# Moving the mix for the gate into the attention part, and splitting the gate's last steps over slots

## The chip, the cores and the metric

The kernel runs on one core of one Trainium2 chip. The metric is the time of one execution on the device, in microseconds, as the median of several runs. The engines are named as the profile names them: PE (TensorE), DVE (VectorE), ACT (ScalarE), POOL (GpSimd) and SP (SyncE, which issues most DMAs here).

## The reference

```python
# attention: batch 8, 12 heads, 448 positions, head size 64
scores = cap * np.tanh(scale * np.matmul(q, k.transpose(0, 1, 3, 2)) / cap)
attn = np.exp(scores - np.max(scores, axis=-1, keepdims=True))
attn = attn / (np.sum(attn, axis=-1, keepdims=True) + 1e-09)
x = np.matmul(attn, v)           # then heads joined: x is (8, 448, 768)
# channel mix
x_prev = np.concatenate([np.zeros((B, 1, D)), x[:, :-1, :]], axis=1)
xk = mu_k * x + (1.0 - mu_k) * x_prev
xr = mu_r * x + (1.0 - mu_r) * x_prev
k = np.maximum(xk @ w_k, 0.0)    # w_k is 768 x 1024
v = k * k @ w_v                  # w_v is 1024 x 768
r = 1.0 / (1.0 + np.exp(-(xr @ w_r)))   # w_r is 768 x 768
return r * v
```

The result of the attention is the x of the second part. Each position is mixed with the position before it, once with mu_k for the keys and once with mu_r for the gate r.

## The kernel before

The kernel works in three stages, one after the other on PE, each engine executing its instructions in the order in which the program was written.

**Attention and keys** (about the first 575 us). There are 48 pairs of heads. Iteration i of the loop calls the steps named in the string STEP one by one, for pair i or a pair one or two behind it. For a pair, PE makes the scores (scores, the tiles s), ACT takes tanh and exp of them (the tiles p), DVE sums them per 32 rows (red, L238), and PE multiplies them with the values (values, the tile pv). The partial sums are gathered by four small DMAs (gather, L243), added and inverted on DVE (recip, L247 to L251), stored and loaded again as a row for all partitions (rec_store, rec_load), and norm (L263) multiplies pv by it: this gives x, 128 features by 448 positions, in one of two tiles. mix_old (ACT, L273) and mix_new (DVE, L278) make xk from x; x_high and x_low (POOL, L74 and L84) split xk into two parts xkh and xkl, from which PE makes the key products seven iterations later (kpart, L313; K in STEP). relu and k_store write them to DRAM as k_d. x_store writes x to DRAM as x_d. Also in this loop, the 44 pieces of the weights are converted: five DVE operations a piece (f in STEP, L372 to L380), one on POOL (L387), and DMAs (weight_load, weight_store to w_d). Iterations 6 to 10 take two pieces, others one, up to about iteration 39.

**Value units** (to about 795 us). v = (k * k) @ w_v is made in 14 units of 256 positions. A unit is a product of 2 x 2 blocks made with seven block products instead of eight (P1 to P7); each of them is a slot. The left operand of a product is a block of the source tile src or a sum or difference of blocks (sums2, on POOL, the tiles s). operand, two slots ahead, splits it into hi (ACT, L553) and lo (DVE, L554), in a ring of three buffers. PE multiplies hi by the high and the low part of the weights and lo by the high part. evacuate then adds the products up from PSUM: p1 (ACT), u2 and u3 (DVE, L588), and four results per unit (DVE, L592, or ACT, for the one that is complete in PSUM), which go to DRAM as v_d. The weights' own blocks and sums are made by w2_prep: those for w_v in the last six iterations of the first loop, those for w_r during the value units.

**Gate units** (to the end). r = sigmoid(xr @ w_r) is made in the same way, in 14 units of seven slots with nine matmuls each. The source is made on the way: src_r_load reads x with the position ahead of it (the tile xc), and src_r, ten slots ahead, multiplies the earlier position by 1 - mu_r (on POOL or ACT in turns, L514 and L516) and adds mu_r times the later one (DVE, L517). In evacuate, ACT applies the sigmoid to each result (L599), POOL multiplies by the value (L600, in the last unit DVE), and SP stores to the output.

A slot wrote its instructions in the order evacuation of the slot before, matmuls, work ahead:

```python
        if g:
            v, r = divmod(g - 1, SLOTS)
            self.evacuate(v, self.products(v)[r])
        if u < 2 * NU:
            self.multiply(u, s)
            self.ahead(g)
```

Of the kernel before, what the change touches and what calls it, by code (L numbers as in the profile page):

```python
# [17 lines left out]
NP = H // 2  # L18
# [33 lines left out]
weight_sum tanh1 exp1 red1 norm recip rec_store K qk_high qk_low tanh2 mix_old mix_new x_high x_low relu k_store  # L52
K exp2 red2 weight_rest weight_sum relu k_store S3 K K tanh3 exp3 red3 relu k_store weight_abs load_qk rec_load x_store weight_store"""
# [6 lines left out]
class Body:  # L60
# [227 lines left out]

    def x_store(self, i):
        self.nc.sync.dma_start(self.x_d[i % NP, :, i // NP, :], self.X[i % 2])  # L290
# [148 lines left out]
    def w2_prep(self, kind):  # L439

        lo = self.W2[kind][1]
        sub = self.nc.gpsimd.tensor_sub
# [24 lines left out]
    def src_v_load(self, u, q):  # L467
        if q == 0:
            self.src[u] = self.srcp.tile([P, NF, 2 * P], F32, name="src")
        self.nc.sync.dma_start(self.src[u][:, 2 * q:2 * q + 2, :],  # L470
                               self.k_d[2 * q:2 * q + 2, :, u * 2 * P:(u + 1) * 2 * P].rearrange("f p t -> p f t"))

    def src_v(self, u, q):
        x = self.src[u][:, 2 * q:2 * q + 2, :]
        self.nc.vector.tensor_mul(x, x, x)  # L475

    def pieces(self, u):

        b, s0 = divmod((u - NU) * 2 * P, S)
        cut = S - s0  # L480
        out = []
        for c in range(2):
            k = cut - c * P
            if k <= 0 or k >= P:
                out.append((c * P, c * P + (k <= 0), P, 1))
            else:
                assert 2 * k == P
                out.append((c * P, c * P, k, 2))
        if out[0][3] == out[1][3] == 1:
            gap = out[1][1] - P  # L490
            return [(0, 0, 2 * P, 1, 0)] if not gap else [(0, 0, P, 2, P + 1)]
        return [(o, i, k, a, k + 1) for o, i, k, a in out]

    def src_r_load(self, u, q):
        b, s0 = divmod((u - NU) * 2 * P, S)
        w = 2 * P + 1 + (s0 + 2 * P > S)
        o = b * (S + 1) + s0
        t = self.xc[u, q] = self.ldp.tile([P, 2 * P + 2], F32, name="xc", bufs=4)
        self.nc.sync.dma_start(t[:, 0:w], self.x_d.rearrange("c p b s -> c p (b s)")[q, :, o:o + w])

    def src_r(self, u, d):
        nc = self.nc
        if d == 0:
# [319 lines left out]
```

## Time and profile before

| | |
|---|---|
| median of 3 runs | 1057.7 us (1057.36 to 1057.74) |
| profiled execution | 1057.44 us |
| its span, first to last instruction | 1055.3 us |
| granted PE clock over the span | 0.955 |
| busy: PE, DVE, ACT, POOL | 930.4, 804.4, 614.2, 576.3 us |

A row of the timeline reads: start in the span, duration, engine, line of the kernel, operation, output and input by the program's names, shapes, count, and in brackets how long the engine sat idle before it and for whom. A row of the groups has the count, then busy us and mean ns of one, then idle time before and its releasers. The chain is the work that ended last, followed back from the end. PEld is PE's loading of weights, SPq and ACTq are the queues on which those engines issue DMAs.

### The profile page before, as it was taken

What the parts mean: (1) busy time and instruction counts of PE and PEld (TensorE: products, weight loads), DVE (VectorE), ACT (ScalarE), POOL (GpSimd) and SP (SyncE); (2) the same over time, 40 slices, a digit from 0 to 9 for tenths busy, and PEclk for the clock granted to TensorE, in tenths of its full rate; (3) what the DMA queues carried; (4) which work ended last, traced back from release to release, by engine and by line L of the source; (5) the groups of instructions that cost most, each with busy time, mean ns of one, the idle gap of its engine ahead of it and who ended that gap; (6) DMA issues with size and microseconds to landing.
All of it is one profiled execution on the core that took longest, in us unless ns stands there. A gap on an engine that the chain in (4) does not pass through costs nothing.

```text
span 1055.3 us, 15510 instructions
## 1 busy us (share of the span) xinstructions
PE 930.4 (88%) x4986; PEld 738.6 (70%) x4986; DVE 804.4 (76%) x1285; ACT 614.2 (58%) x941; POOL 576.3 (55%) x504
## 2 busy tenths in 40 slices
PE   7788989999999999999987999999997667667667
PEld 3345756676767676676666999999997656657556
DVE  7999988878878888766645889999686576575664
ACT  7886768878888888877734343443344333333332
POOL 4756565655556465544145456454466565665662
PEclk9888999999999999999988899999998988998988
DMA  5565556565666656554253544344434344343342
GB/s 155 168 186 186 170 169 214 194 200 192 211 208 204 201 193 211 175 166 129 99 190 130 162 147 123 107 131 131 150 114 145 103 129 128 104 141 116 115 130 92
DMA packets 119546, 164.06 MB, mean 155 GB/s; under 512 B 23072, under 2 KB 103584, under 8 KB 119456
## 3 DMA queue, kind: packets, MB, share of 16 engines
q1 hardware_dynamic: 110240, 148.30, 45.2%
q10 hardware_dynamic: 9216, 14.68, 3.8%
q8 instruction: 41, 0.67, 0.3%
q14 instruction: 49, 0.40, 0.1%
HBM read 106.76 MB, written 53.41 MB: 152 GB/s over the span
## 4 chain that ended last, share of the span: by engine, by line
PE 55%; DVE 14%; issue 11%; POOL 10%; ACT 6%; DMA 2%; SPq 1%; DVEq 0%; ACTq 0%; POOLq 0%
PE ps L569 20%; PE kps L313 16%; PE s L194 9%; PE pv L221 8%; DVE src L517 3%; DVE r L238 3%; POOL src L514 3%; ACT p L212 2%; POOL s L537 2%; PE pv L229 2%; POOL s L533 2%; DVE o L592 1%; ACT p L202 1%; DVE lo L554 1%; POOL o L600 1%
## 5 line engine op out<-in xcount | busy, mean ns | idle before, releaser
L238 DVE TRANSPOSE_TENSOR_REDUCE r<-p 128x28 f32<-128x896 f32 (+1 forms) x240 | 220.1, 922 | 76.2 <-ACT p L212 71.9
L202 ACT ACTIVATE p<-s,scl_t 128x896 f32<-128x896 f32 x192 | 173.4, 903 | 44.6 <-PE s L194 37.0
L212 ACT ACTIVATE p<-p,cap_t 128x896 f32<-128x896 f32 x192 | 182.0, 948 | 10.2 <-ACT ko L320 5.5
L569 PE MATMUL ps<-wrh,hi 128*128 128x384 f32 x294 | 110.4, 375 | 75.9 <-DVE u L588 25.6
L313 PE MATMUL kps<-xkh,wkh 128*128 128x448 f32 x384 | 147.7, 385 | 12.4 <-ACT ko L320 12.4
L313 PE MATMUL kps<-xkl,wkh 128*128 128x448 f32 x384 | 141.9, 370 | 0.5 <-POOL xkl L84 0.5
L313 PE MATMUL kps<-xkh,wkl 128*128 128x448 f32 x384 | 142.0, 370 | 0.0
L569 PE MATMUL ps<-wvh,hi 128*128 128x384 f32 x392 | 132.9, 339 | 4.5 <-ACT hi L553 4.5
L569 PE MATMUL ps<-wvl,hi 128*128 128x384 f32 x392 | 132.4, 338 | 0.0
L387 POOL TENSOR_TENSOR wsq<-wa,wsq 128x384 f32<-128x384 f32 x44 | 44.3, 1007 | 155.9 <-DVE wsq L380 128.1
L221 PE MATMUL pv<-p,rv 128*64 128x448 f32 x576 | 126.6, 577 | 0.0
L569 PEld LDWEIGHTS ps<-wrh,hi 128*128 128x128 f32 x294 | 61.0, 208 | 89.2 <-ACT hi L553 32.5
L84 POOL TENSOR_TENSOR qkl<-rqk,qkh 128x960 fp32r<-128x960 f32 x47 | 106.0, 2256 | 3.9
L554 DVE TENSOR_TENSOR lo<-src,hi 128x512 fp32r<-128x512 f32 (+1 forms) x84 | 79.9, 951 | 36.9 <-ACT hi L553 36.2
L554 DVE TENSOR_TENSOR lo<-s,hi 128x512 fp32r<-128x512 f32 (+1 forms) x112 | 91.0, 813 | 20.3 <-ACT hi L553 20.3
L569 PE MATMUL ps<-wrl,hi 128*128 128x384 f32 x294 | 106.4, 362 | 0.0
L194 PE MATMUL s<-qkh 64*128 64x448 f32 (+1 forms) x336 | 84.6, 444 | 22.6 <-ACT p L202 17.9
L553 ACT CAST hi<-s 128x512 fp32r<-128x512 f32 (+1 forms) x112 | 63.2, 564 | 66.1 <-PE ps L569 47.8
L313 PEld LDWEIGHTS kps<-xkh,wkh 128*128 128x128 f32 x384 | 73.6, 192 | 33.5 <-ACT ko L320 15.3
L600 POOL TENSOR_TENSOR o<-o,vl 128x384 f32<-128x384 f32 x52 | 53.1, 1020 | 74.2 <-ACT o L599 73.5
L194 PEld LDWEIGHTS s<-qkh 64*128 64x128 f32 (+1 forms) x336 | 37.2, 190 | 78.9 <-ACT p L202 28.5
L533 POOL TENSOR_TENSOR s<-src 128x512 f32<-128x512 f32 (+1 forms) x28 | 36.0, 1287 | 103.2 <-DVE src L475 83.8
(95 smaller groups left out, 1968.7 us busy)
## 6 DMA issues: line engine op xcount, KB each, us to landing
rqk<-qk SPq DMA_DIRECT2D x47, 480.0 KB
k_d<-ko ACTq DMA_DIRECT2D x64, 224.0 KB
src<-k_d SPq DMA_DIRECT2D x56, 256.0 KB
rv<-v SPq DMA_DIRECT2D x48, 256.0 KB
x_d<-x SPq DMA_DIRECT2D x48, 224.5 KB
r<-rec_d SPq DMA_DIRECT2D x96, 112.0 KB
v_d<-o SPq DMA_DIRECT2D x56, 192.0 KB
vl<-v_d SPq DMA_DIRECT2D x56, 192.0 KB
```

Source lines behind the costliest of these rows:

```text
L84: {"p": self.nc.gpsimd, "v": self.nc.vector}[e].tensor_sub(*a)
L194: nc.tensor.matmul(s[:, h, 0:S], qk[a][p, k], qk[b][p, 0:S], start=(n == 0), stop=(n == 2))
L202: self.nc.scalar.activation(p32, self.S.pop((i, g))[:, :n, 0:S], AF.Tanh, scale=self.scl_t)
L212: self.nc.scalar.activation(p32, p32, AF.Exp, scale=1.0 if self.maxima else self.cap_t)
L221: nc.tensor.matmul(pv[p, 0:S], v[:, g, h, :], ph[:, h, :], start=(g == 0), stop=False)
L238: self.nc.vector.tensor_reduce(out=out, in_=p32[p, h].rearrange("p h (b k) -> p (h b) k", k=32), axis=mybir.AxisListType.X, op=ALU.add, ap ...
L313: nc.tensor.matmul(self.kps[fc][:, 0:S], w, m[:, dc, :], start=first, stop=last)
L533: pool.tensor_add(s, a(1, 0), a(1, 1))
L553: self.nc.scalar.copy(hi, x)
L554: self.nc.vector.tensor_sub(lo, x, f(hi))
L569: self.nc.tensor.matmul(o, a[:, c, :], w[:, c, :], start=first and k == 0, stop=last and k == len(todo) - 1, skip_group_check=True)
L600: (nc.vector if u == 2 * NU - 1 else nc.gpsimd).tensor_mul(o, o, self.vl.pop((u, key)))
```

## The change

- gate_old (POOL) and gate_new (DVE) make xr, mixed, in the attention loop, in one tile xg, for the pair two behind. They stand after x_low and after red3 in STEP. x_store writes xg instead of x; x_d loses the column for the position ahead of the first.
- The gate units load their source like the value units, three loads of 256 KB a unit; src_r_load, src_r and pieces go.
- A slot writes the matmuls and the work ahead first, then the evacuation of the slot before. The last steps go to a list that is carried out one slot later: the copy and store of a value, and for the gate the sigmoid, into PSUM (tile psg, two buffers), and another slot later the multiplication, now on DVE, with the store.
- The value is loaded two slots ahead of the unit's slot instead of one, into six buffers instead of three.
- The subtractions of w2_prep go from POOL to DVE, for both kinds.

```diff
-weight_sum tanh1 exp1 red1 norm recip rec_store K qk_high qk_low tanh2 mix_old mix_new x_high x_low relu k_store
-K exp2 red2 weight_rest weight_sum relu k_store S3 K K tanh3 exp3 red3 relu k_store weight_abs load_qk rec_load x_store weight_store"""
+weight_sum tanh1 exp1 red1 norm recip rec_store K qk_high qk_low tanh2 mix_old mix_new x_high x_low gate_old relu k_store
+K exp2 red2 weight_rest weight_sum relu k_store S3 K K tanh3 exp3 red3 gate_new relu k_store weight_abs load_qk rec_load x_store weight_store"""
+    def gate_old(self, i):
+        hp = i % NP
+        self.xg = self.up.tile([P, S], F32, name="xg", bufs=1)
+        self.nc.gpsimd.tensor_scalar(self.xg, self.X[i % 2][:, 0:S], self.om["r"][:, hp:hp + 1], None, op0=ALU.mult)
+    def gate_new(self, i):
+        self.nc.vector.scalar_tensor_tensor(out=self.xg, in0=self.X[i % 2][:, 1:], scalar=self.mu["r"][:, i % NP:i % NP + 1],
+                                            in1=self.xg, op0=ALU.mult, op1=ALU.add)
     def x_store(self, i):
-        self.nc.sync.dma_start(self.x_d[i % NP, :, i // NP, :], self.X[i % 2])
+        self.nc.sync.dma_start(self.x_d[i % NP, :, i // NP * S:(i // NP + 1) * S], self.xg)
...
-        sub = self.nc.gpsimd.tensor_sub
+        sub = self.nc.vector.tensor_sub
...
+    def src_load(self, u, q):
...
+        if 2 * q < 2 * self.half(u):
+            x, t = (self.k_d, u) if u < NU else (self.x_d, u - NU)
+            self.nc.sync.dma_start(self.src[u][:, 2 * q:2 * q + 2, :],
+                                   x[2 * q:2 * q + 2, :, t * 2 * P:(t + 1) * 2 * P].rearrange("f p t -> p f t"))
...
-            nc.scalar.activation(o, x, AF.Sigmoid)
-            (nc.vector if u == 2 * NU - 1 else nc.gpsimd).tensor_mul(o, o, self.vl.pop((u, key)))
-            t = ((u - NU) * 2 + key // 2) * P
-            nc.sync.dma_start(self.out[t:t + P, key % 2 * HN:(key % 2 + 1) * HN], o)
+            self.later.append((self.gate if u >= NU else self.value, (u, key, o, x)))
+    def value(self, u, key, o, x):
+        if x is not o:
+            self.nc.scalar.copy(o, x)
+        self.nc.sync.dma_start(self.v_d[u, :, key], o)
+    def gate(self, u, key, o, x):
+        g = self.ps_g.tile([P, 512], F32, name="psg")[:, 0:HN]
+        self.nc.scalar.activation(g, x, AF.Sigmoid)
+        self.later.append((self.out_store, (u, key, o, g)))
+    def out_store(self, u, key, o, g):
+        self.nc.vector.tensor_mul(o, g, self.vl.pop((u, key)))
+        t = ((u - NU) * 2 + key // 2) * P
+        self.nc.sync.dma_start(self.out[t:t + P, key % 2 * HN:(key % 2 + 1) * HN], o)
...
     def slot(self, g):
         u, s = divmod(g, SLOTS)
-        if g:
-            v, r = divmod(g - 1, SLOTS)
-            self.evacuate(v, self.products(v)[r])
         if u < 2 * NU:
             self.multiply(u, s)
             self.ahead(g)
+        now, self.later = self.later, []
+        if g and g <= 2 * NU * SLOTS:
+            v, r = divmod(g - 1, SLOTS)
+            self.evacuate(v, self.products(v)[r])
+        for do, args in now:
+            do(*args)
```

Three places in the order of the instructions. First DVE's queue in one iteration of the attention loop, as it was before (xk is mix_new's, r_ the partial sums of red, wt, wa and wsq the weight preparation, numbered names are buffers):

```order
L278 SCALAR_TENSOR_TENSOR xk<-x_157,mu_k,pv 128x448
L238 TENSOR_REDUCE r_0_189<-p_2_2283 128x28
L238 TENSOR_REDUCE r_0_189<-p_1_2318 64x14 x2
L372 TENSOR_SCALAR wt<-wsq 128x384
L374 TENSOR_SCALAR wa<-wt 128x384
L376 SCALAR_TENSOR_TENSOR wa<-w_2217,wa 128x384
```

After the change the same queue reads there:

```order
L278 SCALAR_TENSOR_TENSOR xk<-x_159,mu_k,pv 128x448
L238 TENSOR_REDUCE r_1_196<-p_2_2207 128x28
L238 TENSOR_REDUCE r_1_196<-p_1_2244 64x14 x2
L295 SCALAR_TENSOR_TENSOR xg<-x_159,mu_r,xg 128x448
L381 TENSOR_SCALAR wt<-wsq 128x384
L383 TENSOR_SCALAR wa<-wt 128x384
```

gate_new (L295) has come between the iteration's last reductions and the weight preparation of the next, and it needs POOL's gate_old.

Second, SP's queue at the seam of two iterations, as it was before (w_d is weight_store's, sq the gathers, rv and w loads):

```order
L259 DMA r<-rec_d_89 64x448 x2
L290 DMA x_d<-x_159 128x449
L406 DMA w_d<-wsq 128x384
L243 DMA sq_200<-r_1_196 32x112 x4
L151 DMA rv<-v 128x512
```

After the change the same queue reads there:

```order
L259 DMA r<-rec_d_89 64x448 x2
L299 DMA x_d<-xg 128x448
L415 DMA w_d<-wsq 128x384
L243 DMA sq_200<-r_1_196 32x112 x4
L151 DMA rv<-v 128x512
```

The places are the same, but the store now has gate_new's xg as its source, and the gathers stand behind it.

Third, DVE's queue over some five slots of a gate unit, as it was before (psg holds the sigmoid, vl the value):

```order
L554 TENSOR_TENSOR lo<-s_9830,hi 128x384
L517 SCALAR_TENSOR_TENSOR src<-xc,mu_r,src 128x256
L592 TENSOR_TENSOR o<-ps_9927,u_9925 128x384
L554 TENSOR_TENSOR lo<-src,hi 128x384
L517 SCALAR_TENSOR_TENSOR src<-xc,mu_r,src 128x256
L592 TENSOR_TENSOR o<-ps_9953,u_9925 128x384
L554 TENSOR_TENSOR lo<-s_9941,hi 128x384
L517 SCALAR_TENSOR_TENSOR src<-xc,mu_r,src 128x256
L592 TENSOR_TENSOR o<-ps_9927,u_9881 128x384
```

After the change the same queue reads there:

```order
L522 TENSOR_TENSOR lo<-src,hi 128x384
L560 TENSOR_TENSOR o<-ps_9832,u_9850 128x384
L575 TENSOR_TENSOR o<-psg,vl 128x384
L522 TENSOR_TENSOR lo<-s_9846,hi 128x384
L560 TENSOR_TENSOR o<-ps_9854,u_9850 128x384
L522 TENSOR_TENSOR lo<-src,hi 128x384
L560 TENSOR_TENSOR o<-ps_9832,u_9812 128x384
L575 TENSOR_TENSOR o<-psg,vl 128x384
L522 TENSOR_TENSOR lo<-s_9868,hi 128x384
L575 TENSOR_TENSOR o<-psg,vl 128x384
```

The mixing (L517) has left DVE's queue here, the multiplication (L575) has come, and a slot begins with its low part, ahead of the addition.

More of the change, by code (lines that the diff above doesn't have):

```diff
@@ L474, in src_v, with square @@
+    def square(self, u, q):
         x = self.src[u][:, 2 * q:2 * q + 2, :]
         self.nc.vector.tensor_mul(x, x, x)
[L477 to L492, printed above, removed]
@@ L593, in evacuate @@
                 x = o
[L594 to L602 removed]
+            self.later.append((self.gate if u >= NU else self.value, (u, key, o, x)))
[11 more added lines that the diff above has]
+        self.nc.sync.dma_start(self.out[t:t + P, key % 2 * HN:(key % 2 + 1) * HN], o)
     def v_load(self, u, key):
[L605 removed]
+        t = self.vl[u, key] = self.ldp.tile([P, HN], F32, name="vl", bufs=6)
         self.nc.sync.dma_start(t, self.v_d[u - NU, :, key])
@@ L650, in step @@
         pair.update(dict.fromkeys("V gather recip rec_store rec_load".split(), i - 1))
-        pair.update(dict.fromkeys("norm mix_old mix_new x_high x_low x_store".split(), i - 2))
+        pair.update(dict.fromkeys("norm mix_old mix_new x_high x_low gate_old gate_new x_store".split(), i - 2))
         for op in STEP.split():
@@ L685, in run @@
             self.k_d = drp.tile([NF, P, NT], F32, name="k_d")
-            self.x_d = drp.tile([ND, P, B, S + 1], F32, name="x_d")
+            self.x_d = drp.tile([ND, P, NT], F32, name="x_d")
             self.rec_d = [drp.tile([2, S], F32, name=f"rec_d{i}") for i in range(NPAIR)]
@@ L719, in run @@
             self.wgen = self.weight_round()
-            self.W2, self.b12, self.src, self.xc, self.ss, self.ops, self.ps, self.ev, self.got, self.vl = ({} for _ in range(10))
+            self.W2, self.b12, self.src, self.ss, self.ops, self.ps, self.ev, self.got, self.vl = ({} for _ in range(9))
             tail = NPAIR + 1
             prepst = ExitStack()
+            self.later = []
             first = -12
@@ L755, in run @@
             self.outp = pool("outp", 4)
+            self.ps_g = pool("psg", 2, space=PSUM)
             self.st = pool("st2", 1, prepst)
@@ L758, in run @@
             prep = self.w2_prep("r")
-            for g in range(2 * NU * SLOTS + 1):
+            for g in range(2 * NU * SLOTS + 3):
                 self.slot(g)
```

49 lines of the change are left out of this document (5 added, 44 removed).

## The prediction

> **What bounds the kernel now.** I read the page's busy row, its 40 slices and the shares of its chain first.
>
> ```profile
> PE 930.4 (88%) x4986; PEld 738.6 (70%) x4986; DVE 804.4 (76%) x1285; ACT 614.2 (58%) x941; POOL 576.3 (55%) x504
> PE   7788989999999999999987999999997667667667
> PEclk9888999999999999999988899999998988998988
> PE 55%; DVE 14%; issue 11%; POOL 10%; ACT 6%; DMA 2%; SPq 1%; DVEq 0%; ACTq 0%; POOLq 0%
> ```
>
> PE is full from about slice 7 to slice 20 (attention with the key products) and again to slice 30 (the value units), and only 60 to 70% busy in the last ten slices (the gate units). Busy time per stage, from the table of windows (start, length, then PE, PEld, DVE, ACT, POOL, granted clock, DMA share):
>
> ```profile
> 70.00:500.00 430.00, 419.94 (x2352) 286.06 (x2349) 348.38 (x587) 343.09 (x439) 238.39 (x205) 0.99 0.59 190
> 585.00:795.00 210.00, 210.00 (x1201) 209.55 (x1201) 183.79 (x264) 86.21 (x162) 107.00 (x78) 0.99 0.43 132
> 795.00:1045.00 250.00, 174.14 (x834) 159.53 (x833) 158.40 (x249) 86.55 (x202) 155.52 (x149) 0.90 0.39 120
> ```
>
> In the gate stage no engine is above 70%. The chain and the timeline say what ends last there:
>
> ```profile
> 584.70 210.13 PE ps L569 x1199
> 859.04 1.33 POOL s L537
> 864.37 1.35 DVE src L517 x2
> 867.80 1.50 POOL src L514 x2
> 862.42 0.52 ACT L599 ACTIVATE o<-o 128x384 f32<-128x384 f32 x1 [4.03 <-DVE o L592]
> 863.03 1.00 POOL L600 TENSOR_TENSOR o<-o,vl 128x384 f32<-128x384 f32 x1 [1.49 <-ACT o L599]
> ```
>
> Up to 794.83 the chain is unbroken PE work. After it, the chain goes round a ring: POOL's sum and mix, DVE's mix, DVE's addition, sigmoid, POOL's multiplication, POOL's next sum. Each engine waits in order for the one before it, and PE starves behind the casts that stand in those queues. This is what the change takes apart.
>
> **The gate stage.** From 794.83 to the span's end it takes 260.5 us. The change removes POOL's multiplication and all mixing from the ring, lets operands go ahead of the evacuation, and spreads sigmoid and multiplication over two later slots. PE then has 14 units x 7 products x 9 matmuls = 882 matmuls. The chain's stretch gives 210.13 / 1199 = 0.1753 us each (its matmuls have the same 384 columns, at a clock of 0.99), so 154.6 us. 1199 is 23 more than the value units' 1176, so 23 x 0.1753 = 4.0 us of that is before 794.83: PE would end at 945.4. The last matmuls and the span's end stand 7.2 us apart now, and the last unit's tail (sigmoid, DVE multiplication, store) keeps its operations:
>
> ```profile
> 1047.46 0.68 PE L569 MATMUL ps<-wrh,lo 128*128 128x384 f32 x3
> ```
>
> Whether PE can run unbroken depends on DVE, which takes over the multiplication. The groups kept apart by shape:
>
> ```profile
> L554 DVE TENSOR_TENSOR lo<-s,hi 128x384 fp32r<-128x384 f32 x56 | 42.0, 751 | 14.8 <-ACT hi L553 14.8
> L554 DVE TENSOR_TENSOR lo<-src,hi 128x384 fp32r<-128x384 f32 x42 | 36.4, 868 | 25.4 <-ACT hi L553 24.8 <-PE ps L569 0.7
> L592 DVE TENSOR_TENSOR o<-ps,u 128x384 f32<-128x384 f32 x84 | 46.1, 549 | 13.2 <-PE ps L569 13.0
> L600 DVE TENSOR_TENSOR o<-o,vl 128x384 f32<-128x384 f32 x4 | 2.1, 558 | 1.8 <-ACT o L599 1.8
> L600 POOL TENSOR_TENSOR o<-o,vl 128x384 f32<-128x384 f32 x52 | 53.1, 1020 | 74.2 <-ACT o L599 73.5
> 863.38 1.07 DVE L554 TENSOR_TENSOR lo<-s,hi 128x384 fp32r<-128x384 f32 x1 [0.99 <-ACT hi L553]
> 869.70 0.55 DVE L554 TENSOR_TENSOR lo<-s,hi 128x384 fp32r<-128x384 f32 x1
> ```
>
> Per unit DVE has 4 x 0.751 + 3 x 0.868 = 5.61 us of low parts, 5 additions from PSUM at 0.549 = 2.75, and 4 multiplications at 0.558 = 2.23: 10.6 us against PE's 11.04, or 96%. The low parts cost 0.55 us alone and 1.07 beside a POOL operation (the last two rows). So DVE's load lies between 8.8 us (all alone) and 12.5 us (all beside POOL); at 12.5 DVE is the bound and the stage is 14 x 1.46 = 20 us longer. The value units show the same construction at 183.79 of 210 us (88%) without a gap in PE. 96% is nearer to that row than to 113%, but with little room, so I add 5 us, with 0 and 20 as ends. ACT (7 casts, 4 sigmoids, 1 copy, at most 0.53 us each: 6.4 us) and POOL (its four sums; 155.52 less what leaves it) have room. On SP a unit has 11 DMAs instead of 14, and the same bytes in some 160 us instead of 250 put the DMA share at 0.39 x 250 / 160 = 0.61, near the attention part's 0.59. The stage becomes 150.6 + 5 + 7.2 = 162.8 us: a gain of 97.7 us.
>
> **The attention part.** Each of the 48 pairs gains one POOL operation (gate_old) and one on DVE (gate_new), and the store of x waits for the latter. The prices come from these rows:
>
> ```profile
> L514 POOL TENSOR_SCALAR src<-xc,om_r 128x256 f32<-128x256 f32 x30 | 30.6, 1026 | 2.6 <-DMA xc<-x_d 2.6
> L514 POOL TENSOR_SCALAR src<-xc,om_r x54: 594/918/1236, 771.3 to 1025.0; 128x256 f32<-128x256 f32 x30, 128x128 f32<-128x128 f32 x24
> L74 POOL TENSOR_SCALAR xkh<-xk 128x448 fp32r<-128x448 f32 x48 | 27.2, 566 | 72.0 <-DVE xk L278 72.0
> L278 DVE SCALAR_TENSOR_TENSOR xk<-x,mu_k,pv 128x448 f32<-128x448 f32 x48 | 30.5, 636 | 1.6 <-ACT pv L273 1.5
> ```
>
> gate_new is 0.64 us (as L278). gate_old has L514's form, a scalar per partition: 0.594 us at 128 columns and 0.918 at 256 are 2.5 ns a column, so 1.40 us at 448. The other end is 0.57 us (L74, same size, constants as scalars). I take 1.40 for its like form. The Trainium skill (GPSIMD Engine Reference, 4.1 Engine selection) calls GpSimd's operations with one input roughly line rate, which would put gate_old beside L74 and the kernel at rival 1's time; L514's 2.5 ns a column against L74's 1.3 speaks against it for this form.
>
> The steady iteration, from DVE's, POOL's and SP's timelines and a piece of the chain:
>
> ```profile
> 221.69 0.59 DVE L247 TENSOR_REDUCE sr<-sq 32x28 f32<-32x448 f32 x1
> 222.80 0.64 DVE L278 SCALAR_TENSOR_TENSOR xk<-x,mu_k,pv 128x448 f32<-128x448 f32 x1
> 223.44 2.52 DVE L238 TRANSPOSE_TENSOR_REDUCE r<-p 128x28 f32<-128x896 f32 x3
> 224.17 1.15 POOL L84 TENSOR_TENSOR xkl<-xk,xkh 128x448 fp32r<-128x448 f32 x1
> 225.35 0.58 SPq L290 DMA_DIRECT2D x_d<-x  x1
> 226.03 0.38 SPq L406 DMA_DIRECT2D w_d<-wsq  x1
> 226.50 2.45 SPq L243 DMA_DIRECT2D sq<-r  x4
> 142.55 1.70 DMA sq<-r
> 177.52 0.59 DVE L263 TENSOR_TENSOR x<-pv,r 128x448 f32<-128x448 f32 x1
> 537.50 0.63 DVE L263 TENSOR_TENSOR x<-pv,r 128x448 f32<-128x448 f32 x1 [4.26 <-DMA r<-rec_d]
> ```
>
> The last two rows are 34 iterations apart: 10.59 us each, set by PE. The change closes a new ring: xk (ends 223.44), POOL's two parts to 225.32 (1.88 us), gate_old 1.40, gate_new 0.64, then SP: from the store of x to the last of the four gathers queued behind it 225.35 to 228.95 (3.60), landing 1.70, then DVE's sum to the end of xk 1.75. Together 10.97 us, some 0.4 over PE's 10.59; DVE also waits about 0.8 us for gate_old behind its reductions (225.96 against 226.72), with everything on its queue. Over the 24 steady iterations that still prepare weights (2.2 us of DVE each) 0.3 to 0.4 us gives some 7 us with part of it absorbed; the ends are 0 (gate_old at 0.57: ring 10.1) and 14. Later iterations have no weight work and no store of weights ahead of the gathers (226.50 - 226.03 = 0.5 us less in the ring), and cost nothing.
>
> Before about 150 us DVE already sets the pace:
>
> ```profile
> 120.00:140.00 20.00, 16.24 (x86) 10.17 (x86) 19.32 (x33) 15.16 (x21) 12.52 (x13) 0.95 0.57 181
> ```
>
> Eleven such iterations hold the new work: 11 x 0.64 = 7 us, plus gate_old's 0.8 us wait in the first five, less what neighbours absorb: 9 us, ends 4 and 14.
>
> **The bridge between attention and value units.** The 16 subtractions of the weight preparation go from POOL to DVE. PE is stopped there by casts and copies that stand behind them:
>
> ```profile
> 547.30 0.74 PE L313 MATMUL kps<-xkh,wkh 128*128 128x448 f32 x1 [4.67 <-ACT ko L320]
> 570.35 0.47 PE L313 MATMUL kps<-xkh,wkh 128*128 128x448 f32 x1 [2.90 <-ACT ko L320]
> 580.32 0.69 PE L569 MATMUL ps<-wvh,hi 128*128 128x384 f32 x1 [4.48 <-ACT hi L553]
> ```
>
> These stalls make 12 us. On DVE such a subtraction costs 0.55 us alone instead of POOL's 1.02 (L600, the same shape), and the handover to POOL and back goes; I take half, 6 us, with ends 0 and 10. The twelve subtractions for the gate weights fall in the value units, where the twelve mixing operations of the first gate units leave DVE: nothing, as PE sets the end there; if that cover were gone, 12 x 0.55 = 7 us.
>
> **The sum.** Span 1055.3 - 97.7 + 7 + 9 - 6 = 967.6 us; the profiled execution took 1057.44, 2.1 more than its span, so 969.7, said as 970. (The median of the runs is 1057.7, 0.3 above that execution.)
>
> **Rivals.**
> 1. The attention part hides the new work: gate_old at 0.57 us, no ring above 10.59, and only some 5 us in the DVE-paced start. 970 - 7 - 4 = 959 us. For it: L74. Against it: L514's form.
> 2. DVE becomes the bound of the gate stage, each low part beside a POOL sum at 1.07 us: 20 us instead of 5, so 985. For it: 96% load. Against it: POOL keeps only four sums in a unit of seven low parts.
> 3. Slower: the slots do not overlap. The cast waits for PE to free one of three operand buffers, and low part, addition and multiplication follow in order: 0.51 + 1.07 + 0.55 + 0.56 = 2.7 us a slot, 18.8 a unit, 14 x 18.8 + 7.2 - 4 = 266 us in the stage, so 970 + 104 = 1074. It decides from 18 us a unit on, when DVE's lag of a slot does not hide the cast. Against it: the value units have the same three buffers and order and no gap.
> 4. The change doesn't do what it says: casts still stand behind the sigmoid, which now waits for DVE's addition of the slot before, and half the gate stage's gain is lost: about 1019 us.
>
> **Chances.** Forecast as told 0.62 (its own range 957 to 982), rival 1 0.17, rival 2 0.15, rival 3 0.03, rival 4 0.03. The range 951 to 989 takes in the first three. A difference under 0.2% (2 us) can't be told from none here; faster holds all but rival 3 and a little: 0.96, same 0.01, slower 0.03.
>
> **What would show it.** Gate stage right: PE unbroken in the chain to within 10 us of the end, granted clock near 0.99 there, units of 11 to 11.5 us, DVE above 90%. Attention: xg on POOL at 1.4 us, DVE waiting for it, an iteration of 10.8 to 11 us up to about 440. Bridge: the stalls of 4.67, 2.90 and 4.48 us about halved. Wrong if PE's idle time in the gate stage names ACT or DVE for more than 20 us, or if the gathers behind the store of x are late by more than a microsecond in each iteration.

## The result, and the profile after

| | before | after |
|---|---|---|
| median of the runs (4 each) | 1057.53 us | 1001.39 us (998.11 to 1003.34) |
| profiled execution, span | 1057.44, 1055.3 us | 998.11, 995.8 us |
| ratio of the times | | 0.9468, 95% interval 0.9442 to 0.9494 |

The change makes the kernel 5.3% faster. The forecast was 970 us with a range to 989, so 31 us of the expected 88 are missing. From the page of the changed kernel: the busy row, PE's row over 40 slices, and the chain's shares by engine.

```profile
PE 914.0 (92%) x4986; PEld 722.7 (73%) x4986; DVE 801.2 (80%) x1305; ACT 600.7 (60%) x887; POOL 500.8 (50%) x418
PE   7778779999999999999999777999999999999997
PE 37%; DVE 22%; POOL 10%; DMA 10%; issue 9%; SPq 5%; ACT 5%; ACTq 0%; DVEq 0%; POOLq 0%
```

PE's slices are full to the end now, so PE no longer starves in the gate stage. But the chain has become 22% DVE where it was 14%, and PE's share fell from 55% to 37%: something with DVE in it now sets the pace in places where PE did. The windows (start, length, then PE, PEld, DVE, ACT, POOL, granted clock, DMA share) show one such place:

```profile
70.00:500.00 430.00, 409.95 (x2270) 276.27 (x2267) 368.76 (x622) 332.24 (x425) 287.86 (x238) 0.98 0.57 185
605.00:815.00 210.00, 196.78 (x1098) 191.05 (x1097) 171.43 (x240) 76.90 (x139) 75.78 (x52) 0.99 0.38 122
832.00:985.00 153.00, 147.10 (x833) 143.32 (x832) 121.29 (x211) 75.50 (x158) 54.39 (x51) 1.00 0.62 197
```

The second row lies in the value units. Before, 210 us there held 210.00 us and 1201 matmuls of PE; now they hold 196.78 and 1098. The stages are cut by DVE's normalisations of the first, the 13th and the last pair, and by PE's first matmul of the value units and of the gate units. In the timelines of before, the first and the 13th normalisation and the first gate matmul (the last normalisation and the first value matmul stand in the prediction):

```profile
29.29 0.59 DVE L263 TENSOR_TENSOR x<-pv,r 128x448 f32<-128x448 f32 x1
166.10 0.59 DVE L263 TENSOR_TENSOR x<-pv,r 128x448 f32<-128x448 f32 x1
789.38 0.33 PE L569 MATMUL ps<-wrh,hi 128*128 128x384 f32 x1
```

In the timelines of after, all five:

```profile
29.55 0.59 DVE L263 TENSOR_TENSOR x<-pv,r 128x448 f32<-128x448 f32 x1
181.47 0.59 DVE L263 TENSOR_TENSOR x<-pv,r 128x448 f32<-128x448 f32 x1
557.72 0.62 DVE L263 TENSOR_TENSOR x<-pv,r 128x448 f32<-128x448 f32 x1 [0.54 <-DMA r<-rec_d]
600.87 0.69 PE L537 MATMUL ps<-wvh,hi 128*128 128x384 f32 x1 [8.94 <-ACT hi L521]
826.69 0.33 PE L537 MATMUL ps<-wrh,hi 128*128 128x384 f32 x1
```

| stage | before, us | after, us | measured | forecast |
|---|---|---|---|---|
| early attention (1st to 13th normalisation) | 136.8 | 151.9 | +15.1 | +9 |
| rest of the attention (13th to last) | 371.4 | 376.3 | +4.9 | +7 |
| bridge (last normalisation to first value matmul) | 42.8 | 43.2 | +0.4 | -6 |
| value units | 209.1 | 225.8 | +16.7 | 0 |
| gate units to the span's end | 265.9 | 169.1 | -96.8 | -97.7 |

With the 0.3 us ahead of the first normalisation the measured column makes the span's 59.5 us. The gate stage came out within a microsecond of its term; the value units, priced at nothing, are the largest miss.

**What stops PE in the value units.** The table of waits for PE from 600 to 990 us (total, times, longest) has as its first row:

```profile
PE ps L537 <- DVE o L560: 16.9, 25, 1.7
```

The piece of the timelines of DVE, POOL and PE around the longest of these waits:

```profile
677.31 1.48 POOL L503 TENSOR_TENSOR s<-s,src 128x512 f32<-128x512 f32 x1
677.68 1.53 DVE L456 TENSOR_TENSOR u<-wrl,u 128x384 f32<-128x384 f32 x1
678.75 1.60 POOL L505 TENSOR_TENSOR s<-src 128x512 f32<-128x512 f32 x1
679.13 1.64 DVE L446 TENSOR_TENSOR wrl<-wrl,wrh 128x384 fp32r<-128x384 f32 x1
682.36 1.58 DVE L522 TENSOR_TENSOR lo<-src,hi 128x512 fp32r<-128x512 f32 x1
683.87 0.55 DVE L560 TENSOR_TENSOR o<-ps,u 128x384 f32<-128x384 f32 x1
684.56 0.41 PE L537 MATMUL ps<-wvh,hi 128*128 128x384 f32 x1 [1.70 <-DVE o L560]
```

PE waits not for an operand but for an evacuation: L560, the addition for key 3, which reads the PSUM bank of P5. P3 accumulates into that same bank, and only one product (P4) stands between the two. So the addition has one slot to be done: 2.08 us in a value unit, 1.56 in a gate unit. Ahead of it on DVE now stand the low part L522, which the change's "operands first" put there, and, further up, the weight subtractions that came over from POOL (L456 here). The low part itself took 1.58 us here, beside one of POOL's sums, while one of the same size, at 681.29, took 0.68; what POOL's sums add to the wait was not tested by itself. The same thing happens once in nearly every gate unit, by a smaller amount:

```profile
903.87 0.51 ACT L521 CAST hi<-src 128x384 fp32r<-128x384 f32 x1 [0.62 <-PE ps L537]
904.10 0.55 DVE L556 TENSOR_TENSOR u<-ps,p 128x384 f32<-128x384 f32 x1
904.32 1.01 POOL L507 TENSOR_TENSOR s<-src,s 128x384 f32<-128x384 f32 x1 [0.56 <-DVE lo L522]
904.57 1.18 DVE L522 TENSOR_TENSOR lo<-src,hi 128x384 fp32r<-128x384 f32 x1
905.67 0.54 DVE L560 TENSOR_TENSOR o<-ps,u 128x384 f32<-128x384 f32 x1
906.36 0.42 PE L537 MATMUL ps<-wrh,hi 128*128 128x384 f32 x1 [0.45 <-DVE o L560]
```

A gate unit takes 11.62 us, of which seven slots of 1.56 are 10.92; the 0.70 go with this wait. (The row counts 0.45 us as idle: it takes a matmul as busy for 0.34 us, although the next one starts after 0.17.) That is 9.1 us in 13 units; the last unit has another order of products and waits 0.31 us.

**What holds up the attention.** DVE's and POOL's timelines in an early iteration:

```profile
57.38 1.41 POOL L292 TENSOR_SCALAR xg<-x,om_r 128x448 f32<-128x448 f32 x1
58.82 0.69 DVE L295 SCALAR_TENSOR_TENSOR xg<-x,mu_r,xg 128x448 f32<-128x448 f32 x1 [1.43 <-POOL xg L292]
61.66 0.56 DVE L389 SCALAR_TENSOR_TENSOR wsq<-w,wt 128x384 f32<-128x384 uint32 x1
62.31 1.01 POOL L396 TENSOR_TENSOR wsq<-wa,wsq 128x384 f32<-128x384 f32 x1 [3.52 <-DVE wsq L389]
```

The group of DVE's second half of the mix over all 48 pairs (busy, mean ns, then idle time ahead of it):

```profile
L295 DVE SCALAR_TENSOR_TENSOR xg<-x,mu_r,xg 128x448 f32<-128x448 f32 x48 | 33.8, 703 | 26.2 <-POOL xg L292 25.7
```

POOL's operation takes the 1.40 us that the prediction estimated, but it comes at the end of POOL's queue, DVE waits 1.43 us for it (not 0.8), DVE's weight operations stand behind, and POOL's next weight sum (L396) waits for the last of them. That is a ring of DVE and POOL, and the first four iterations go from 9.6 us in the mean to 11.5. In the later pairs PE waits a few times for the eviction of a key product. The tables of waits from the 13th to the last normalisation, before and after:

```profile
PE kps L313 <- ACT ko L320: 0.3, 1, 0.3
PE kps L322 <- ACT ko L329: 5.1, 5, 1.8
```

That is the size of the stage's loss of 4.9 us. In one of these waits a late normalisation holds up ACT's L273, and the key product's eviction stands behind that; the timelines of ACT and PE:

```profile
182.10 0.64 ACT L273 ACTIVATE pv<-x,om_k 128x448 f32<-128x448 f32 x1 [1.85 <-DVE x L263]
183.60 0.95 ACT L329 ACTIVATE ko<-kps 128x448 f32<-128x448 f32 x2
184.18 0.47 PE L322 MATMUL kps<-xkh,wkh 128*128 128x448 f32 x1 [1.75 <-ACT ko L329]
```

### The profile page after: what moved, and what is told of

Same layout as the page of the kernel before. It is cut to its first block, busy times and chain, and to the rows that moved or that the text cites. A ratio compares the mean times of both kernels' runs of the same rounds, so it can differ in the third digit from the quotient of the medians.

```text
span 995.8 us, 15130 instructions
## 1 busy us (share of the span) xinstructions
PE 914.0 (92%) x4986; PEld 722.7 (73%) x4986; DVE 801.2 (80%) x1305; ACT 600.7 (60%) x887; POOL 500.8 (50%) x418
## 4 chain that ended last, share of the span: by engine, by line
PE 37%; DVE 22%; POOL 10%; DMA 10%; issue 9%; SPq 5%; ACT 5%; ACTq 0%; DVEq 0%; POOLq 0%
PE ps L537 25%; PE kps L322 6%; DMA sq<-r 4%; SPq L243 4%; PE s L194 3%; DVE r L238 3%; DVE lo L522 3%; POOL xg L292 3%; PE pv L221 3%; DMA src<-x_d 3%; POOL xkl L84 2%; DVE xg L295 2%; ACT p L212 2%; POOL qkl L84 2%; DVE o L560 1%
## 5 line engine op out<-in xcount | busy, mean ns | idle before, releaser
L501 POOL TENSOR_TENSOR s<-src 128x512 f32<-128x512 f32 (+1 forms) x28 | 32.6, 1166 | 251.9 <-DVE src L486 154.9
L537 PE MATMUL ps<-wvh,hi 128*128 128x384 f32 x392 | 135.3, 345 | 22.2 <-DVE o L560 11.1
L221 PE MATMUL pv<-p,rv 128*64 128x448 f32 x576 | 132.0, 598 | 0.0
L522 DVE TENSOR_TENSOR lo<-s,hi 128x512 fp32r<-128x512 f32 (+1 forms) x112 | 82.5, 737 | 48.9 <-ACT hi L521 32.1
L396 POOL TENSOR_TENSOR wsq<-wa,wsq 128x384 f32<-128x384 f32 x44 | 44.6, 1014 | 133.9 <-DVE wsq L389 133.9
L521 ACT CAST hi<-src 128x512 fp32r<-128x512 f32 (+1 forms) x84 | 47.7, 568 | 100.3 <-PE ps L537 83.3
L537 PE MATMUL ps<-wrh,hi 128*128 128x384 f32 x294 | 99.9, 340 | 6.2 <-DVE o L560 5.8
L537 PE MATMUL ps<-wrl,hi 128*128 128x384 f32 x294 | 98.7, 336 | 0.0
L522 DVE TENSOR_TENSOR lo<-src,hi 128x512 fp32r<-128x512 f32 (+1 forms) x84 | 74.1, 882 | 28.4 <-PE ps L537 15.1
L537 PEld LDWEIGHTS ps<-wvh,hi 128*128 128x128 f32 x392 | 75.0, 191 | 28.3 <-ACT hi L521 14.7
```

What stands on the lines that cost most here:

```text
L221: nc.tensor.matmul(pv[p, 0:S], v[:, g, h, :], ph[:, h, :], start=(g == 0), stop=False)
L396: {"p": self.nc.gpsimd, "v": self.nc.vector}[e].tensor_add(sq, f(a), sq)
L521: self.nc.scalar.copy(hi, x)
L522: self.nc.vector.tensor_sub(lo, x, f(hi))
L537: self.nc.tensor.matmul(o, a[:, c, :], w[:, c, :], start=first and k == 0, stop=last and k == len(todo) - 1, skip_group_check=True)
```

## Experiments

The kernel before took 1053.96, 1055.94 and 1058.33 us (medians) beside the three groups of runs, so kernels are compared by their ratio to it. The value and gate columns are the stages of the profiled execution, cut as above; the next two columns are the median value unit and gate unit, from the first matmul of one unit to that of the next.

| kernel | ratio (95% interval) | median, us | value units | gate | value unit | gate unit |
|---|---|---|---|---|---|---|
| the change | 0.9468 (0.9442 to 0.9494) | 1001.4 | 225.8 | 169.1 | 15.9 | 11.62 |
| evacuation first | 0.9291 (0.9273 to 0.9310) | 979.9 | 214.5 | 159.7 | 15.0 | 10.92 |
| order of products | 0.9371 (0.9353 to 0.9389) | 988.7 | 214.7 | 169.2 | 14.9 | 11.62 |
| subtractions on POOL | 0.9431 (0.9414 to 0.9448) | 994.0 | 216.7 | 168.6 | 15.1 | 11.63 |
| mix's first half on ACT | 0.9467 (0.9449 to 0.9485) | 998.1 | 226.1 | 169.7 | 15.9 | 11.61 |
| store of x late | 0.9500 (0.9467 to 0.9533) | 1002.7 | 226.0 | 170.3 | 15.9 | 11.63 |
| mix's second half late | 0.9381 (0.9350 to 0.9412) | 989.8 | 225.9 | 170.0 | 15.9 | 11.62 |
| inline sigmoid | 0.9664 (0.9632 to 0.9697) | 1020.6 | 226.1 | 190.5 | 15.9 | 13.13 |
| inline, evacuation first | 0.9422 (0.9408 to 0.9437) | 997.0 | 214.4 | 176.8 | 15.0 | 12.16 |
| evacuation first, part on POOL | 0.9193 (0.9161 to 0.9226) | 971.1 | 206.7 | 159.5 | 14.56 | 10.92 |
| evacuation first, all on POOL | 0.9215 (0.9200 to 0.9229) | 976.0 | 208.5 | 160.3 | 14.56 | 10.92 |
| the helpful edits together | 0.9079 (0.9067 to 0.9092) | 961.0 | 206.6 | 160.8 | 14.56 | 10.92 |

**Evacuation first.** The theory is that the addition's place behind the low part, together with the shared bank, costs the value units; the rivals are DVE's added load, and that the old order is needed.

```
     def slot(self, g):
         u, s = divmod(g, SLOTS)
-        if u < 2 * NU:
-            self.multiply(u, s)
-            self.ahead(g)
         now, self.later = self.later, []
         ...
             self.evacuate(v, self.products(v)[r])
+        if u < 2 * NU:
+            self.multiply(u, s)
+            self.ahead(g)
         for do, args in now:
```

> The changed kernel with the slot's order turned back: the evacuation of the slot before is written ahead of the multiplication and of the operands' casts, low parts and sums; the deferred sigmoid and multiplication stay where they are. Stages meant here: value units = first value matmul to first gate matmul (209.1 us before, 225.8 after the change), gate = first gate matmul to the span's end (265.9 and 169.1). Theory A (P3 accumulates into the PSUM bank of P5, so TensorE waits for DVE's addition for key 3, and 'operands first' puts this addition behind the low part and the weight preparation): the addition comes out in time again, value units 209 to 213 us, a gate unit 11.0 us instead of 11.6, gate stage 160 to 164, time about 976. Theory B (the weight subtractions that moved to DVE slow the value units, whatever the order): value units stay at 220 or more, time 990 or more. Theory C (the old order brings the gate stage's ring back, since casts stand behind additions): gate stage over 180 us, time over 1000.

A window of this run in the gate stage:

```profile
820.00:970.00 150.00, 150.00 (x867) 149.94 (x867) 122.94 (x217) 75.58 (x164) 58.53 (x52) 1.00 0.64 203
```

What is left of the waits for key 3 (same table as above):

```profile
PE ps L537 <- DVE o L560: 6.9, 6, 1.7
```

The gate stage is unbroken PE work (150.00 of 150 us, units of 10.92). The value units fall by 11.3 us to 214.5, somewhat less than theory A said (209 to 213): while gate weights are prepared, one unit in three takes 14.56 and the others 15.4 and 16.5; the last ones, without that work, take 14.56. So A holds in the gate stage and for most of the value units, something of B is left, and C is wrong: the new operations' order, not the old one, was the worse.

**Order of products.** The same bank, tested without touching any engine's load or the order of operands and evacuation.

```
-        return (P1, P6, P2, P7, P5, P4, P3) if u < 2 * NU - 1 else (P1, P6, P5, P7, P4, P3, P2)
+        return (P1, P6, P5, P7, P4, P2, P3) if u < 2 * NU - 1 else (P1, P6, P5, P7, P4, P3, P2)
         ...
-            self.v_load(u, {0: 0, 2: 3, 3: 2, 4: 1}[s])
+            self.v_load(u, {0: 3, 2: 2, 3: 0, 4: 1}[s])
```

> The changed kernel with only the order of a unit's seven products changed, from P1 P6 P2 P7 P5 P4 P3 to P1 P6 P5 P7 P4 P2 P3, and the loads of the value tiles in the order in which the keys now come. Operands stay first and all weight preparation stays on DVE. Key 3's addition can now start after P7, and two products (P4, P2) instead of one stand between it and P3, which accumulates into the bank that it reads. Theory A (the shared bank): one slot more of room ends nearly all of the wait, value units 209 to 214 us, gate unit 11.0 to 11.2 us, gate stage 160 to 164, time about 977. Theory B (DVE's added load is the cause): no change, value units 222 or more and time within 4 us of 1000, since DVE has the same work in the same queue.

PE's waits for DVE from 600 to 990 us:

```profile
PE ps L537 <- DVE u L556: 7.9, 13, 2.4
PE ps L537 <- DVE o L560: 1.2, 4, 0.3
```

The one wait of a gate unit in its timeline:

```profile
905.79 0.41 PE L537 MATMUL ps<-wrh,hi 128*128 128x384 f32 x1 [0.46 <-DVE u L556]
```

In the value units theory A is right, if a little short of its 209 to 214 us: with two products between P5 and P3 they lose 11.1 us although DVE has the same work. In the gate units the expectation failed in an instructive way: still 11.62, and so 988.7 us instead of about 977. The wait for key 3 is all but gone (16.9 to 1.2 us), but its place is taken by L556, the addition that reads the bank of P6 ahead of P7. In this order the low part that runs long beside POOL's sum stands ahead of the addition for the pair P6, P7, which has one product between it, now as before. A wait of one bank moved to another.

**Subtractions on POOL.**

```
-        sub = self.nc.vector.tensor_sub
+        sub = self.nc.gpsimd.tensor_sub
```

> The changed kernel with the weight preparation's 28 subtractions (16 for the value weights, 12 for the gate weights) on POOL again as before the change. The operands stay first. Theory A: the value units recover in part only, since the addition still stands behind the low parts: 214 to 220 us, the slot ahead of P3 at 2.4 us or more instead of 2.08, gate stage unchanged at 169; time about 990. Theory B (the subtractions on DVE are the whole cause): value units 209 to 212 us, time about 983. On the bridge (last normalisation to the first value matmul, 43 us with either kernel): if the move to DVE gained or lost anything there it shows as a difference of more than 1 us; I expect less than 3 us either way.

The value units recover 9.1 of 16.7 us and the gate units nothing. That is theory A as put here (214 to 220 us); theory B (209 to 212) is refuted. So neither the order nor the subtractions are the whole cause: both stand in one queue ahead of the addition. The bridge came to 45.1 us against 43.2.

**Evacuation first, part or all of the subtractions on POOL.** Here the 12 subtractions for the gate weights, which fall in the value units, are on POOL, and the 16 for the value weights stay on DVE; in a second kernel all 28 are on POOL.

```
-        sub = self.nc.vector.tensor_sub
+        sub = (self.nc.vector if kind == "v" else self.nc.gpsimd).tensor_sub
```

> The changed kernel with the evacuation ahead of multiplication and operands (as in the run that gave 979.9 us) and the 12 subtractions for the gate weights on POOL again; the 16 for the value weights, at the bridge, stay on DVE. Theory A+ (what the evacuation's order left in the value units, 214.6 against 209.1 us, is DVE's queue in the units that prepare gate weights: each such subtraction of 0.55 to 1.6 us stands ahead of an addition): value units 209 to 211, gate stage 159.7 unchanged, bridge 43, time about 975. Rival (what is left comes from elsewhere, such as the first unit): value units 213 or more, time 979 or more.

> The run of 971.1 us (evacuation first, subtractions for the gate weights on POOL) with the 16 subtractions for the value weights on POOL too, so that the move of the subtractions to DVE is wholly undone. It prices the bridge by itself: from the last normalisation to the start of the second value unit, 62.2 us before the change, 64.1 after it, 61.5 in the run of 971.1. If the move to DVE gained there what the prediction said (6 us), 66 to 69 us and a time near 977; if it gained little, 61 to 64 us and a time within 3 us of 971.

PE's waits in the value and gate units of the first kernel: one, ahead of the first matmul.

```profile
PE ps L537 <- ACT hi L521: 8.9, 1, 8.9
```

All value units but the first take 14.56 us in both kernels, and all gate units but the last 10.92. The two causes together are the whole loss in these stages; in the first kernel the value units even came out below the 209 to 211 us of theory A+, as the first unit was shorter too (17.45 us against 19.40 before). The four combinations can now be compared in the units 2 to 14, in which the bridge has no part: 189.3 us with the evacuation first and all subtractions on POOL, 196.3 with the operands first instead, 197.7 with the subtractions on DVE instead, and 204.9 with both, as in the change. So the order alone costs 7.0 us there, the subtractions alone 8.4, and both 15.6: they add up.

The second kernel prices the bridge: from the last normalisation to the second value unit 63.4 us against 61.5. The move to DVE is worth some 1.8 us there, not 6; the second kernel's 976.0 us is more than 3 us from 971.1, but by their ratios the two kernels can't be told apart (intervals 0.9161 to 0.9226 and 0.9200 to 0.9229).

**Inline sigmoid, with operands or evacuation first.** In both, the gate units have the sigmoid and the POOL multiplication straight behind the addition; in the second, the evacuation is first as well.

```
-            self.later.append((self.gate if u >= NU else self.value, (u, key, o, x)))
+            if u >= NU:
+                nc.scalar.activation(o, x, AF.Sigmoid)
+                (nc.vector if u == 2 * NU - 1 else nc.gpsimd).tensor_mul(o, o, self.vl.pop((u, key)))
+                t = ((u - NU) * 2 + key // 2) * P
+                nc.sync.dma_start(self.out[t:t + P, key % 2 * HN:(key % 2 + 1) * HN], o)
+                continue
+            self.later.append((self.value, (u, key, o, x)))
```

> The changed kernel with the sigmoid and the last multiplication of the gate units made inside the evacuation again, at once behind the addition, the multiplication on POOL and the sigmoid's result in SBUF, as before the change. The mix stays in the attention part, the operands stay ahead of the evacuation. It tells which part of the change carried the gate stage's gain (265.9 to 169.1 us, a unit from some 19.5 to 11.62). Theory M (the mixing on ACT, DVE and POOL was the ring; without it the inline sigmoid and multiplication fit): gate stage at most 175 us, time at most 1004. Theory S (the cast of a later slot standing behind the sigmoid, which waits for DVE's addition, is as large a part): a slot with an output costs some 2.1 to 2.6 us instead of 1.56, gate stage 185 to 205, time 1015 to 1035.

> The changed kernel with two of its three parts undone for the gate units: evacuation ahead of the operands, and sigmoid and POOL multiplication inline behind the addition. What is left of the change there is the mix made in the attention part. Beside the earlier runs it completes a table of order (operands first or evacuation first) by sigmoid (inline or a slot later): gate units of 11.62 (operands first, later), 10.92 (evacuation first, later) and 13.1 (operands first, inline). Theory S (the inline sigmoid stands in front of the next cast, and with the evacuation first it does so in the same slot): units of 13 to 15 us, gate stage 188 to 215, time 1003 to 1030. Theory M (the mixing was nearly all of the old ring, and evacuation first is the better order here too): units under 12.5 us, gate stage under 182, time under 1000.

ACT's and PE's timelines of the second kernel in a gate unit:

```profile
904.52 0.53 ACT L563 ACTIVATE o<-o 128x384 f32<-128x384 f32 x1 [1.60 <-DVE o L560]
904.95 0.49 ACT L521 CAST hi<-src 128x384 fp32r<-128x384 f32 x1
905.35 0.47 ACT L554 COPY p<-ps 128x384 f32<-128x384 f32 x1
905.87 0.44 PE L537 MATMUL ps<-wrh,hi 128*128 128x384 f32 x1 [0.81 <-ACT p L554]
```

The sigmoid waits 1.6 us for DVE, and the cast and the copy of P1 behind it wait with it; PE needs that copy, since P2 accumulates into the bank of P1. This completes a table of the gate stage: 265.9 us before; 176.8 with the mix in the attention part, and the loads that go with it, alone; 159.7 with the later sigmoid and multiplication added; 169.1 with the operands first added. Added in this order, the mix carried 89.1 us, the later sigmoid and multiplication 17.1, and the operands first took 9.4 back. In the first of the two runs theory S stood (190.5, inside its 185 to 205); in the second theory M did (176.8 and 997 us).

**The first half of the mix on ACT.**

```
-        self.nc.gpsimd.tensor_scalar(self.xg, self.X[i % 2][:, 0:S], self.om["r"][:, hp:hp + 1], None, op0=ALU.mult)
+        self.nc.scalar.mul(self.xg, self.X[i % 2][:, 0:S], self.om["r"][:, hp:hp + 1])
```

> The changed kernel with the first half of the gate mix in the attention part (the multiplication by 1 - mu, one a pair) on ACT instead of POOL. Theory P (in the early pairs, which still prepare weights, a ring DVE - POOL sets the pace: POOL's squares, high and low parts and this 1.40 us operation, then DVE's second half, then DVE's weight work, which waits for and feeds POOL): without 1.40 us on POOL the early iterations of 11.5 us become about 10, the last normalisation starts at 546 to 551 us instead of 557.7, time about 990. Theory D (DVE's own second half, 0.7 us a pair, is the cause): last normalisation at 554 or later, time within 3 us of 1000.

The groups of the two halves:

```profile
L295 DVE SCALAR_TENSOR_TENSOR xg<-x,mu_r,xg 128x448 f32<-128x448 f32 x48 | 33.8, 704 | 0.7
L292 ACT ACTIVATE xg<-x,om_r 128x448 f32<-128x448 f32 x48 | 31.5, 656 | 0.0
```

DVE's idle time there is gone (26.2 to 0.7 us), and the first five iterations take 10.6 to 10.7 us instead of 11.5, some 0.9 of the added 1.9 us. The rest stays. The early part falls from 151.9 to 147.2 us, but the later pairs take 381.6 us from the 13th to the last normalisation, where the kernels with an untouched attention part show 376.3 to 381.1, and the time does not change. Theory D's figures came true (last normalisation at 558.5 us, time 998.1) and theory P's did not, although the wait that P named cost time in the early pairs. What ACT's added 31.5 us do to the later pairs was not taken apart.

**The second half of the mix, or only its store, a step later.** The first kernel moves the store of x behind the next iteration's gathers; the second moves DVE's half and the store there, with two buffers (gate_late takes the pair one step later, and gate_last the last pair at its old place). The edit of the second:

```
-STEP = """gather load_v weight_load more weight_low S0 S1 V S2 f f f f f tanh0 exp0 red0
+STEP = """gather load_v weight_load more weight_low S0 S1 V S2 f f f f f tanh0 exp0 red0 gate_late
...
-K exp2 red2 weight_rest weight_sum relu k_store S3 K K tanh3 exp3 red3 gate_new relu k_store weight_abs load_qk rec_load x_store weight_store"""
+K exp2 red2 weight_rest weight_sum relu k_store S3 K K tanh3 exp3 red3 gate_last relu k_store weight_abs load_qk rec_load weight_store"""
+    def gate_late(self, i):
+        if i < NPAIR - 1:
+            self.gate_new(i)
+            self.x_store(i)
...
```

> The changed kernel with only the store of a pair's gate input moved on SP: behind the next iteration's four gathers instead of ahead of them. The measure is the time from the 13th to the last normalisation (371.4 us before the change, 376.3 after, 376 to 380 in the runs so far) and from the first to the 13th (136.8 and 151.9). Theory S (the ring the prediction named: the store waits on SP for DVE's second half of the mix, and the gathers behind it start the next iteration's sums late): 13th to last falls to 371 to 373 us, first to 13th stays at 151 to 152, time about 993. Theory L (the added work on POOL and DVE itself costs the time): both unchanged, time within 3 us of 998.

> The changed kernel with the second half of the gate mix (DVE) and its store moved into the next iteration, behind its gathers and its first reductions; two buffers for the mixed tile instead of one. No operation changes its engine. Theory W (in the early pairs DVE stands still 1.4 us an iteration for POOL's first half, which comes late behind POOL's weight work, and POOL's next weight work then waits for DVE; in the steady pairs SP's store holds the gathers): first to 13th normalisation 142 to 146 us instead of 151.9, 13th to last 371 to 374 instead of 376.3, time 984 to 988. Theory D (DVE's own 0.7 us an operation fills the iteration): first to 13th 149 or more, time 994 or more.

The group of DVE's half with the late mix:

```profile
L295 DVE SCALAR_TENSOR_TENSOR xg<-x,mu_r,xg 128x448 f32<-128x448 f32 x48 | 34.2, 713 | 6.6 <-POOL xg L292 6.6
```

PE's timeline at the bridge with the late store:

```profile
571.93 0.74 PE L330 MATMUL kps<-xkh,wkh 128*128 128x448 f32 x1 [10.36 <-ACT ko L337]
```

The late mix did what theory W said: DVE's wait falls from 26.2 to 6.6 us, the early part from 151.9 to 145.4, the rest from 376.3 to 373.8, and the ratio from 0.9468 to 0.9381; the time, 989.8 us, lies a little above its 984 to 988. DVE still has 12 operations of 0.7 us more than before in the early part, 8.4 us, and 8.6 of the 15.1 us stay there: so the wait was some 6.5 of them, and the rest fits DVE's own work. The late store alone missed theory S: 375.1 in the rest instead of 371 to 373, a little under the 376.3 to 381.1 of the kernels with an untouched attention part, and no better time. Its bridge grew to 48.0 us: on SP the last but one store stood behind the loads of the value weights, and POOL's last first half waits for the one buffer, which that store reads.

What makes the later pairs slower stays open in part. With the late store DVE's wait there for the gathers fell from 6.4 to 1.3 us, but PE's wait for the key evictions only from 5.1 to 4.7, so the store's place on SP is not the main carrier. With the first half on ACT DVE no longer waited for it, and PE's wait was 8.8 us; with the late mix it was 2.7. The gains of the late store (1.1 us) and of the late mix (2.5 us) in this stage are smaller than the 4.8 us by which kernels with the same attention part differ.

**Together.** Evacuation first, gate weights' subtractions on POOL, late mix.

> The edits that helped, together: evacuation ahead of the operands, the 12 subtractions for the gate weights on POOL, the second half of the gate mix and its store in the next iteration. If the two causes (the addition behind the low part in the units; DVE's wait for the first half of the mix in the attention part) are apart in place and time, their gains add: attention as in the run with the late mix (last normalisation near 549 us instead of 557 to 562), value units 207 and gate stage 159.5 as in the run of 971.1 us, time 960 to 963. If they share a cause, the time stays above 966.

Windows in the value and gate units of this kernel:

```profile
600.00:790.00 190.00, 190.00 (x1098) 190.00 (x1098) 163.72 (x227) 75.04 (x138) 99.34 (x65) 1.00 0.41 128
800.00:950.00 150.00, 150.00 (x868) 149.94 (x867) 122.89 (x217) 75.65 (x164) 58.45 (x52) 1.00 0.64 203
```

PE is busy for 340 of 340 us there, and the last normalisation starts at 548.5 us. The gains add, as expected (960.99 us, ratio 0.9079). It beats both kernels of this case: by 9.2% the one before and by some 4% the changed one.

## Why the prediction was right or wrong

- **Gate stage, right in its sum, not in its inner split, and the near hit is luck.** The term was -97.7, the measurement -96.8. The 5 us put in for DVE's low parts were 9.4 us of waits for the shared bank (gone with the evacuation first, 159.7 us). The sum's matmuls and tail were some 3.5 us too long and hid that: at 794.83 us 32 of the gate's matmuls were done in the trace of before, not 23, since nine of the value units' had run before 584.70; and a gate unit's 63 matmuls took 10.92 us, 0.1733 each instead of 0.1753. DVE was not at 96%: it was busy for 121.29 of 153 us, 79%, in the window above, or 9.2 us a unit instead of 10.6. The prediction counted "operands ahead of the evacuation" as part of the gain; it cost 9.4 us.
- **The step that failed: "nothing, as PE sets the end there" for the value units.** It looked at DVE's total load and at the row of 210.00 us, not at the order of DVE's queue: it never asked which of DVE's operations PE waits for inside a slot. What the runs showed in its place: PE waits for the addition for key 3, which has one slot, and both halves of the change put work ahead of it on DVE, the order (7.0 us in the units 2 to 14) and the subtractions (8.4 us). They cost 15.6 us together there, and 16.7 in the whole stage. The fallback price, 12 x 0.55 = 7 us, took the time of a subtraction alone; beside POOL's sums one took 1.53.
- **Early attention, mis-sized: +15.1 against 9.** The operation's price was right (1.41 against 1.40 us), the wait wrong (1.43 against 0.8 in an iteration), and that POOL's next weight work depends on DVE's was missed. The late mix, which takes this wait away, recovers 6.5 us.
- **Later attention, +4.9 against 7 (up to +9.7 in the kernels that left this part as it is): a size that fits, by another way.** The prediction spread 0.3 to 0.4 us over 24 iterations; PE's loss came in five waits for ACT's key evictions, 5.1 us in all. The ring through SP's store and gathers was not the main carrier: moving that store left 4.7 us of them. What delays those evictions is open.
- **Bridge, +0.4 against -6.** The move to DVE gives 1.8 us. The rest was assumed from halving the stalls of 4.67, 2.90 and 4.48 us, but they became two, of 5.01 and 8.94. The first subtraction stands on DVE behind the last pair's second half of the mix, which waits for POOL, and ACT's cast, ahead of the key eviction, waits for that subtraction:

```profile
563.04 0.68 DVE L295 SCALAR_TENSOR_TENSOR xg<-x,mu_r,xg 128x448 f32<-128x448 f32 x1 [3.31 <-POOL xg L292]
563.64 0.55 DVE L455 TENSOR_TENSOR u<-p,wvl 128x384 f32<-128x384 f32 x1
564.23 0.51 ACT L445 CAST wvh<-u 128x384 fp32r<-128x384 f32 x1 [3.38 <-DVE u L455]
567.77 0.74 PE L322 MATMUL kps<-xkh,wkh 128*128 128x448 f32 x1 [5.01 <-ACT ko L329]
```

- **The sum:** 16.7 (value units), 6.4 (bridge), 6.1 less 2.1 (attention), 0.9 (gate) and the 0.3 ahead of it make 28 us; the profiled execution is another 3.3 below the median. All terms' errors but one went the same way, and the largest stood in a term that was put at nothing; the range's end of 989 us took in rival 2, a miss in the gate stage alone.
- **The rivals:** none of the four happened. DVE as the bound of the gate stage is refuted by its 79%; with the sigmoid and multiplication straight behind the addition the stage took 17.1 us more, and the later steps took this away. The Trainium skill's rule on one-input operations (GPSIMD Engine Reference, 4.1 Engine selection), which stood beside rival 1, is not borne out for this form: 1.417 us on POOL against 0.656 on ACT for the same operation.

## What to carry to other kernels

Before an operation is put ahead of an evacuation, list which product next writes each PSUM bank and how many products stand between: an evacuation that has only one slot must be early in its engine's queue, and what is moved to that engine must not stand ahead of it, even when the engine has time to spare (DVE was busy for 171 of 210 us where PE lost most). The Trainium skill (Perfetto Trace Analysis, Matmuls) asks that independent matmul groups rotate through banks so that evacuation overlaps; the runs agree: this kernel lets two products share a bank with one product between, and PE stopped at P5 and P3 in the change, at P6 and P7 in the other order of products, and at P1 and P2 with the inline sigmoid and evacuation first. And an in-place sum split over two engines can be begun on one engine and ended on the other an iteration later: here that took DVE's idle time ahead of the second half from 26.2 to 6.6 us without moving any work to another engine.

## What was not expected of the hardware

A DVE operation with two inputs in SBUF does not merely run slower beside one of POOL's sums, which has two inputs too; it ends a fixed time after it. In the rows above POOL's sums end at 678.79, 680.35 and 905.33, and DVE's operations that started beside them end at 679.21, 680.77 and 905.75: 0.42 us later each time, whenever they started. In the whole trace of the change, all 48 such operations of 384 columns that took over 0.6 us end 0.41 to 0.42 us after POOL's, and the 24 of 512 columns that took over 0.75 us end 0.55 us after it. So such an operation, 0.55 us alone, cost 1.18 to 1.64 in these rows, by how much of POOL's was left. The addition at 904.10, with one input in PSUM, overlapped POOL's sum from 904.32 and took 0.55 as ever. The Trainium skill (SBUF — State Buffer, SBUF: two separate sides) says that the pair of ports is locked for the whole instruction and that the other engine fully blocks; these rows agree with it.
